# Products in 64-row tiles beside a windowed attention, sums of v in 64x32 tiles, and queues listed by hand

## The chip, the cores and the metric

One core of a Trainium2 chip runs the whole kernel as one program. The metric is the device time in microseconds, the median of three runs. All tensors are float32. The wide products use the fp32r form, in which a float32 operand is split beforehand into a high part (hi) and a rest (lo) and a product is the sum of three (hi*hi, hi*lo, lo*hi); the program lists them as TERMS.

## The reference

```python
x = A_x                                            # 2048 rows of 512
g = sigmoid((x * gate_w).sum(-1, keepdims=True))
a_ = x @ dft_hid_re.T ; b_ = x @ dft_hid_im.T      # 512 x 512 each
a = dft_seq_re @ a_ - dft_seq_im @ b_              # 2048 x 2048 each
qkv = x @ wqkv                                     # 32 heads of 16 columns
scores = q @ k.T * 0.25                            # query i sees keys i-255 .. i
b = softmax(scores) @ v @ wo
out = g * a + (1 - g) * b
```

## The kernel before

**Wide products.** Every product that is not attention has 128 contracted rows, 128 columns of weights and 512 streamed columns. Projections of q, k and v (`qk_proj`, `v_proj`) and the hidden transform (`ab_proj`) take 12 such products for one result of 128x512 in PSUM; the sequence transform (`c_block`, `c_half`, line 534) takes 48 for each of 16 row blocks, first with the real matrix, then with the imaginary one. The matrices come in 64 pieces of 128x1024, loaded by SP's queue into `raw` and split into `hi` (a cast) and `lo` (a subtraction) in halves of 512 columns by "jobs" that are dealt out one by one between the products. Results of the first half of the transform go to DRAM (`r_scr`) and are loaded again to be added to the second (`add`, `add_r`). In all these are 2490 products of 512 columns.

**Attention.** Heads go in 4 groups of 8; queries and keys in 32 blocks of 64 a group, so 128 blocks n. In each, 4 pairs of heads p. `s_pair` (line 372) takes the 64 queries of two heads as 128 weight columns: `make_pad` (lines 353, 355) copies them with zeros into `pad`, so that the heads stay apart in the contraction; 320 keys stream by. VectorE adds the mask and takes the row's extreme (line 374), ScalarE takes the exponential and its row sum (line 377). Maxima go through a transpose (`ml_split`, `ml_turn`, `ml_rows`) and DRAM into extra rows of `ring`, so that `t_pair` (line 454), 19 blocks later (LAG), makes the same scores transposed, key rows by query columns, with the maximum already taken off; ScalarE takes the exponential into `pt` (line 455) and GpSimd clears what lies outside the window (lines 459, 463). Every 4 to 6 blocks `pv` (line 480) sums v over the keys in 128x32 tiles, four column tiles beside one another, in plain float32, for which the profile has two records an instruction; v is spread with zeros into `vpad` by GpSimd (line 437). The sums are divided by the row sums when they leave PSUM (line 501).

**End.** `wo_begin` and `wo_end` multiply the attention's output with wo by a scheme with seven products of 128x256 columns for each pair of row blocks (line 929, 336 instructions), between the last blocks of the transform.

**What sets the order.** TensorE's order is the program's own: the loop over n puts S, T and two rations of `fill` (steps of the generator `dense`, one wide product each) behind one another. The other engines' instructions are ordered by the tile scheduler's timeline model, held in places by `behind`. PSUM has 8 banks: four for `s` and `t` (pool `ps_a`, one bank each), two for `o`, two for the wide products.

```python
ps = ps_a.tile([P, 512], F32, name="s", tag="st")                                          # 371
nc.tensor.matmul(ps[:, :w], PAD[0, n][:, p], ring[1][:, p, k0:k0 + w], start=True, stop=True)   # 372
```

Of the kernel before, what the change touches and what calls it, by code (L numbers as in the profile page):

```python
# [19 lines left out]
NP = 4  # L20
BQ = 64
NB = S // BQ
WIN = 320
BIG = 1e30
SCALE = 0.25
LAG = 19
WARM = 10
SWITCH = 6
FILL_FIRST, FILL_PAIR, FILL_T = 3.0, 4.0, 3.0
# [3 lines left out]
def fnet_window_mix(ctx: ExitStack, tc: tile.TileContext, xT, x, wqk, wv, wr, wi, cr, ci, wo, gw, out):  # L33
# [4 lines left out]
    st = ctx.enter_context(tc.tile_pool(name="st", bufs=3))  # L38
    ev = ctx.enter_context(tc.tile_pool(name="ev", bufs=5))
# [6 lines left out]
    qk_scr = [[[dram.tile([2, P, 512], F32, name=f"qk_scr{i}_{g}_{c}") for c in range(4)]  # L46
               for g in range(NG)] for i in range(2)]
    v_scr = [dram.tile([2, P, 2, NG, 64], F32, name=f"v_scr{i}") for i in range(8)]
    ab_scr = [[dram.tile([P, 2, D], F32, name=f"ab_scr{i}_{c}") for c in range(n)] for i, n in enumerate((4, 16))]
    m_scr = [dram.tile([4, NP, 512], F32, name=f"m_scr{i}") for i in range(16)]  # L50
    l_scr = [dram.tile([NP, 2, 512], F32, name=f"l_scr{i}") for i in range(16)]
    o_scr = [dram.tile([NG, P, 512], F32, name=f"o_scr{i}") for i in range(4)]
    r_scr = [[dram.tile([P, D], F32, name=f"r_scr{i}_{c}") for c in range(16)] for i in range(3)]

    def ld(dst, src):
        mark("sp", nc.sync.dma_start(dst, src))

# [4 lines left out]
    last = {}  # L62

# [3 lines left out]
    @contextmanager  # L67
    def behind(*engines):
        with ExitStack() as es:
            for e in engines:  # L70
                if e in last:
                    es.enter_context(tc.issue_after(last[e]))
            yield
# [13 lines left out]
    def split_psum(hi, lo, ps, scale=1.0):  # L87
        mark("act", nc.scalar.activation(hi, ps, AF.Copy, scale=scale))
        if scale == 1.0:
            mark("dve", nc.vector.tensor_sub(lo, ps, f(hi)))  # L90
        else:
            mark("dve", nc.vector.scalar_tensor_tensor(lo, ps, scale, f(hi), op0=OP.mult, op1=OP.subtract))
# [3 lines left out]
    def load_raw(src):  # L96
        raw = st.tile([P, 1024], F32, name="raw", bufs=2)
        ld(raw, src)
        return raw
# [9 lines left out]
    ended = []  # L109
# [1010 lines left out]
```

## Time and profile before

| | |
|---|---|
| runs (us) | 844.39, 843.87, 844.32; median 844.32 |
| profiled execution | span 841.8 us from its first to its last instruction, 2.5 us under the median of the runs (no time of its own is listed beside the span) |
| TensorE (PE) | 837.9 us busy, granted clock full throughout |
| VectorE (DVE), ScalarE (ACT), GpSimd (POOL) | 643.1, 610.1, 294.9 us busy |
| transfers | 161.03 MB, SP's queue 58.9% of the 16 engines' span |

A product's duration in the profile (393 ns for 512 columns) overlaps the next product's; what counts on the path is the distance from start to start. The chain of waits follows the last instruction back, and its shares add up to the span.

### The profile page before, as it was taken

The page shows a single profiled execution, that of the slowest core. Times are in us where ns is not written, and L with a number is a line of the kernel's source. Part 1 is how long each engine was busy: PE and PEld are TensorE (multiplying, and loading weights), DVE is VectorE, ACT ScalarE, POOL GpSimd, SP SyncE. Part 2 cuts the span into 40 slices and gives each one's busy share as a digit, 9 for nine tenths or more (in the row PEclk, how much of TensorE's full clock was granted, in tenths as well). Part 3 has the DMA queues.
Part 4 walks back from the last instruction along what each step waited for, and adds up shares of the span by engine and source line. Part 5 has one row for each costly group of instructions (what it writes and reads, how often), then busy time and mean ns, then how long its engine had stood idle before and what let it go on. Part 6 is the DMA issues. An engine that isn't in the chain of part 4 may idle for free.

```text
span 841.8 us, 17198 instructions
## 1 busy us (share of the span) xinstructions
PE 837.9 (100%) x5322; PEld 698.4 (83%) x5322; DVE 643.1 (76%) x2084; ACT 610.1 (72%) x1832; POOL 294.9 (35%) x604
## 2 busy tenths in 40 slices
PE   9999999999999999999999999999999999999998
PEld 8888888888888888888888887878888878878997
DVE  5588977777879787787877876878987867656974
ACT  6488888878888897787877877867877865553330
POOL 8101333233332233342323243343143357756410
PEclk9999999999999999999999999999999999999999
DMA  8776678485756183533454557969864256456632
GB/s 301 249 225 205 209 237 282 158 273 194 231 206 197 46 235 111 175 116 122 140 163 124 167 160 221 299 217 317 277 200 155 96 175 196 143 195 203 206 133 93
DMA packets 94491, 161.03 MB, mean 191 GB/s; under 512 B 26816, under 2 KB 35520, under 8 KB 94400
## 3 DMA queue, kind: packets, MB, share of 16 engines
q1 hardware_dynamic: 93968, 159.28, 58.9%
q8 instruction: 42, 0.69, 0.3%
q10 hardware_dynamic: 432, 0.66, 0.2%
q14 instruction: 49, 0.40, 0.1%
HBM read 108.27 MB, written 51.64 MB: 190 GB/s over the span
## 4 chain that ended last, share of the span: by engine, by line
PE 100%; DVE 0%; issue 0%
PE dc L534 42%; PE dab L309 11%; PE dqk L286 10%; PE t L454 9%; PE s L372 9%; PE o L480 8%; PE dv L309 5%; PE t L929 5%; PE s L274 1%; PE dv L599 1%; PE s L392 0%; PE t L564 0%; DVE rt L566 0%
## 5 line engine op out<-in xcount | busy, mean ns | idle before, releaser
L534 PE MATMUL dc<-big,hi 128*128 128x512 f32 x1020 | 344.3, 393 | 0.0
L374 DVE CUSTOM_DVE_ANT_0 sm<-s,mask 128x320 f32<-128x320 f32 (+4 forms) x512 | 235.1, 464 | 111.0 <-PE s L372 71.1
L377 ACT ACTIVATE sm<-sm,ml 128x320 f32<-128x320 f32 (+4 forms) x512 | 277.3, 543 | 56.2 <-DVE ml L374 52.4
L455 ACT ACTIVATE pt<-t 128x320 f32<-128x320 f32 (+4 forms) x392 | 159.5, 411 | 83.5 <-PE t L454 78.2
L534 PE MATMUL dc<-big,lo 128*128 128x512 f32 x510 | 200.0, 392 | 0.0
L534 PEld LDWEIGHTS dc<-big,hi 128*128 128x128 f32 x1020 | 179.4, 188 | 21.2
L459 POOL TENSOR_SCALAR_AFFINE_SELECT pt<-pt 128x128 f32<-128x128 f32 x196 | 75.7, 386 | 278.2 <-ACT pt L455 276.1
L454 PE MATMUL t<-ring,pad 128*128 128x320 f32 (+4 forms) x512 | 156.6, 306 | 0.0
L372 PE MATMUL s<-ring,pad 128*128 128x320 f32 (+4 forms) x512 | 155.0, 303 | 0.0
L355 DVE TENSOR_SCALAR pad<-ring,half 96x256 fp32r<-96x256 f32 x384 | 118.7, 356 | 5.2 <-PE t L454 4.9
L454 PEld LDWEIGHTS t<-ring,pad 128*128 128x128 f32 x512 | 96.0, 188 | 30.4 <-issue 8.7
L372 PEld LDWEIGHTS s<-ring,pad 128*128 128x128 f32 x512 | 96.2, 188 | 20.3 <-DVE ml L374 0.7
L534 PEld LDWEIGHTS dc<-big,lo 128*128 128x128 f32 x510 | 95.9, 188 | 11.9
L593 DVE TENSOR_TENSOR lo<-raw,hi 128x512 fp32r<-128x512 f32 x139 | 95.9, 697 | 2.5 <-ACT hi L593 2.4
L377 ACT ACTIVATION_READ_ACCUMULATOR sm<-sm,ml 128x1 f32 x512 | 97.3, 190 | 0.0
L309 PE MATMUL dab<-hi,big 128*128 128x512 f32 x256 | 88.9, 394 | 0.0
L286 PE MATMUL dqk<-big,hi 128*128 128x512 f32 x240 | 85.0, 393 | 0.0
L437 POOL TENSOR_SCALAR vpad<-vr,half 128x256 f32<-128x256 f32 x64 | 62.1, 981 | 60.4 <-PE o L480 29.5
L353 ACT ACTIVATE pad<-ring,half 96x256 fp32r<-96x256 f32 x128 | 66.8, 522 | 0.0
L459 POOL TENSOR_SCALAR_AFFINE_SELECT home<-home 128x128 f32<-128x128 f32 x60 | 33.9, 565 | 89.8 <-ACT home L455 85.3
L463 POOL TENSOR_SCALAR_AFFINE_SELECT pt<-pt 128x128 f32<-128x128 f32 x172 | 63.0, 366 | 0.0
L593 DVE CAST hi<-raw 128x512 fp32r<-128x512 f32 x126 | 53.9, 435 | 11.9 <-PE dc L534 10.6
(121 smaller groups left out, 1034.0 us busy)
## 6 DMA issues: line engine op xcount, KB each, us to landing
qk_scr<-home SPq DMA_DIRECT2D x32, 512.0 KB
ring<-qk_scr SPq DMA_DIRECT2D x32, 512.0 KB
raw<-cr SPq DMA_DIRECT2D x32, 512.0 KB
raw<-ci SPq DMA_DIRECT2D x32, 512.0 KB
r_scr<-ev SPq DMA_DIRECT2D x42, 256.0 KB
ab_scr<-home SPq DMA_DIRECT2D x20, 512.0 KB
big<-ab_scr SPq DMA_DIRECT2D x20, 512.0 KB
ring<-qk_scr SPq DMA_DIRECT2D x32, 256.0 KB
```

The lines of the kernel that those rows point to most:

```text
L286: nc.tensor.matmul(ps, w[a][:, c:c + 128], XT[dk, ss][:, b], start=n == 0, stop=n == 11)
L309: nc.tensor.matmul(ps, XT[dk, ss][:, a, c * 128:(c + 1) * 128], wh[b], start=n == 0, stop=n == 11)
L355: mark(f"pad{i}", nc.vector.tensor_scalar(dst, src, half[:96, h:h + 1], None, op0=OP.mult))
L372: nc.tensor.matmul(ps[:, :w], PAD[0, n][:, p], ring[1][:, p, k0:k0 + w], start=True, stop=True)
L374: mark("dve", nc.vector.tensor_tensor_reduce(out=sm[:, :w], in0=ps[:, :w], in1=mask[:, WIN - w:], scale=1.0, scalar=3e38, op0=OP.add, op1= ...
L377: mark("act", nc.scalar.activation(sm[:, :w], sm[:, :w], AF.Exp, bias=nm[:, c], scale=-1.0, accum_out=l[:, c]))
L454: nc.tensor.matmul(ps[:, :w], PAD[1, n][:, p], ring[0][:, p, q0:q0 + w], start=True, stop=True)
L455: nc.scalar.activation(pt[:, p, :w], ps[:, :w], AF.Exp, scale=-1.0)
L459: nc.gpsimd.affine_select(a, a, pattern=[[0, 2], [2, 64]], compare_op=OP.is_ge, fill=0.0, base=1, channel_multiplier=-1)
L480: nc.tensor.matmul(OT[g, sb][32 * p:32 * p + 32, q - sb * 512:e - sb * 512], v2[:, p], pt[:, p, q - q0:e - q0], start=first, stop=kb == 8 ...
L534: nc.tensor.matmul(ps, w[a][:, i % 8 * 128:i % 8 * 128 + 128], ab[SC[i]][:, b], start=i == ends[0] and a + b == 0, stop=i == ends[1] and a ...
L593: return fn(*args)
```

## The change

**Tiles of the wide products.** From the q and k projections of rows 1024 on to the seventh block of the second transform, `product` issues each wide product as two of 64 contracted rows, `lhs[r]` and `rhs[r]` with r the rows 0-63 or 64-127. `halves64` pairs them: at step t the upper half of one result, and beside it the lower half of another result, in another bank, from an order that is rotated and 6 steps late (DELAY). A result is ready when both halves are through. Between the halves a `tick`, a ScalarE copy of one column of the bank, orders them. 24 products at the start, 96 behind them and 426 at the end (LATE: the last nine blocks, `c_block`) keep 128 rows; 1944 are halved.

**Attention.** Blocks are of 128 queries or keys, 8 groups of 4 heads, LAG 9 blocks. Each head has 48 rows of `ring` at partition 0 or 64 (its 16 columns three times, as hi or lo), with the maxima behind them in two more; the scores of two heads are two products of 64 rows (384 columns, two banks of one PSUM tile), with no `pad`. S keeps only the extreme (VectorE writes the scores to `junk`); its exponential and row sum are gone. T takes one exponential of 128x768 for two heads. `pv` sums v in 64x32 tiles (64 keys, 16 columns of v and 16 ones, which give the row sums); two halves of keys go to two banks, ScalarE copies both out (`o_evict`), VectorE adds them, and the inverse row sums travel through DRAM (`l_move` to `l_back`) before GpSimd multiplies (`o_mul`).

**Queues.** All five engines' orders are now the program's: `agenda` lists by quarter block when each step is issued, `due` by product steps. Of the transforms' inputs 50 pieces, x, weights and the copies of the hidden transform are loaded by GpSimd's queue; 21 of the first transform's partial results are added in DRAM by accumulating transfers, in place of a load and an add. The hidden transform's results are stored once as float32 and split again after loading (`load_ab`). `hi` casts of pieces go to ScalarE, `lo` to VectorE, after attention to GpSimd. PSUM: two tiles of two banks (`ps_a`) for S, T, `o` and the transposes, four banks for wide products. SWITCH goes from 6 to 7. The first pair's copy of a wo product is VectorE's instead of ScalarE's.

```diff
-LAG = 19
+LAG = 9
+VISIT = 4
+DELAY = 6
+LATE = 9
-    ps_a = ctx.enter_context(tc.tile_pool(name="ps_a", bufs=4, space=PSUM))
-    ps_o = ctx.enter_context(tc.tile_pool(name="ps_o", bufs=2, space=PSUM))
-    ps_d = ctx.enter_context(tc.tile_pool(name="ps_d", bufs=2, space=PSUM))
+    ps_a = ctx.enter_context(tc.tile_pool(name="ps_a", bufs=2, space=PSUM))
+    ps_d = ctx.enter_context(tc.tile_pool(name="ps_d", bufs=4, space=PSUM))
...
     def s_pair(n, p):
...
-        ps = ps_a.tile([P, 512], F32, name="s", tag="st")
-        nc.tensor.matmul(ps[:, :w], PAD[0, n][:, p], ring[1][:, p, k0:k0 + w], start=True, stop=True)
-        sm = at.tile([P, WIN], F32, name="sm", bufs=3)
-        mark("dve", nc.vector.tensor_tensor_reduce(out=sm[:, :w], in0=ps[:, :w], in1=mask[:, WIN - w:],
...
-        mark("act", nc.scalar.activation(sm[:, :w], sm[:, :w], AF.Exp, bias=nm[:, c], scale=-1.0,
-                                         accum_out=l[:, c]))
+        ps = ps_a.tile([P, 2, 512], F32, name="s", tag="st")
+        for h in range(2):
+            r = slice(64 * h, 64 * h + 48)
+            nc.tensor.matmul(ps[:, h, :w], ring[0][r, p, j * P:j * P + P], ring[1][r, p, k0:k0 + w],
+                             start=True, stop=True)
+        for h in range(2):
+            c = p * 8 + h * 4 + jj
+            mark("dve", nc.vector.tensor_tensor_reduce(out=junk[:, :w], in0=ps[:, h, :w], in1=mask[:, WIN - w:],
...
     def t_pair(n, p):
...
-        nc.tensor.matmul(ps[:, :w], PAD[1, n][:, p], ring[0][:, p, q0:q0 + w], start=True, stop=True)
-        nc.scalar.activation(pt[:, p, :w], ps[:, :w], AF.Exp, scale=-1.0)
+        ps = ps_a.tile([P, 2, 512], F32, name="t", tag="st")
+        for h in range(2):
+            r = slice(64 * h, 64 * h + 50)
+            nc.tensor.matmul(ps[:, h, :w], ring[1][r, p, q0:q0 + P], ring[0][r, p, q0:q0 + w],
+                             start=True, stop=True)
+        ph = slice(2 * p, 2 * p + 2)
+        nc.scalar.activation(pt[:, ph, :w], ps[:, :, :w], AF.Exp, scale=-1.0)
...
-            for p in range(NP):
-                nc.tensor.matmul(OT[g, sb][32 * p:32 * p + 32, q - sb * 512:e - sb * 512], v2[:, p],
-                                 pt[:, p, q - q0:e - q0], start=first, stop=kb == 8 * sb + 7,
-                                 skip_group_check=True)
+        for n, pair in enumerate(pairs):
+            for h, (kb, _) in enumerate(pair):
+                a, e = spans[kb, h]
+                r = slice(64 * h, 64 * h + 64)
+                v = vt[(4 * G + kb // 4) % 3]
+                for j in range(HG):
+                    nc.tensor.matmul(o[32 * j:32 * j + 32, h, a - q0:e - q0], v[r, kb % 4, 32 * j:32 * j + 32],
+                                     PT[G * NB + kb][r, j, a - kb * P:e - kb * P],
+                                     start=n == 0, stop=n == len(pairs) - 1, skip_group_check=True)
...
+    def product(part, half, i):
...
+        r = slice(64 * half, 64 * half + 64)
+        nc.tensor.matmul(o.ps, lhs[r], rhs[r], start=start, stop=end and o.left == 0, skip_group_check=True)
+        if end:
+            if o.left:
+                nc.scalar.copy(tick, o.ps[:, 0:1])
+            else:
+                o.end(o)
+    def halves64(groups):
+        first = [(p, i) for g in groups for p in g for i in range(p.n)]
+        second = [(p, i) for g in groups for p in [g[-1], *g[:-1]] for i in range(p.n)]
...
+        for t in range(len(first) + DELAY):
...
+                product(part, 0, i)
+            if t >= DELAY:
+                part_b, i_b = second[t - DELAY]
+                product(part_b, 1, i_b)
+            if t < len(first):
+                job(i + 1)
+            beat()
+            yield
...
+            after(STORE, add_pool if tb in sent else ld, r_scr[0][tb], t)
...
-        nc.scalar.copy(u, p1)
+            after(1, nc.scalar.copy if i else nc.vector.tensor_copy, u, p1)
```

TensorE in the middle of the run, before: S and T (lines 372, 454) alternate behind two transform products each.

```order
L372 MATMUL s_6956<-ring1_265,pad0_1_261 128x320
L534 MATMUL dc_6901<-big_3725,hi_6804 128x512
L534 MATMUL dc_6901<-big_3725,lo_6805 128x512
L454 MATMUL t_6964<-ring0_264,pad1_0_262 128x320
L534 MATMUL dc_6901<-big_3791,hi_6804 128x512 x2
L372 MATMUL s_6969<-ring1_265,pad0_1_261 128x320
```

The same stage in the changed kernel; d_5604 and d_4964 are two results whose upper and lower halves go side by side (line 553), and the two heads of S or T are the row with x2 (lines 373, 432).

```order
L373 MATMUL s_5611<-ring1_270,ring0_269 128x384 x2
L553 MATMUL d_5604<-big_4211,lo_5339 128x512
L553 MATMUL d_4964<-big_5151,lo_5228 128x512
L553 MATMUL d_5604<-big_4275,hi_5338 128x512
L553 MATMUL d_4964<-big_5185,hi_5227 128x512
```

One more pair with the names of the last two rows follows, and then T: where two whole products stood between S and T, three pairs of half products or four stand now.

TensorE at a visit of `pv`, before (two results o, since 64-key blocks cross the border of 512 queries):

```order
L480 MATMUL o_4438<-pt_4538,vpad0_299 32x320 x4
L480 MATMUL o_4438<-pt_4598,vpad1_300 32x256 x4
L480 MATMUL o_4894<-pt_4598,vpad1_300 32x64 x4
L480 MATMUL o_4438<-home_304,vpad1_300 32x192 x4
L480 MATMUL o_4894<-home_304,vpad1_300 32x128 x4
```

and now, one result a visit, with equal widths for the two halves of rows:

```order
L467 MATMUL o_4126<-pt_3877,vt0_286 32x320 x8
L467 MATMUL o_4126<-pt_3942,vt0_286 32x256 x4
L467 MATMUL o_4126<-pt_3700,vt2_288 32x256 x4
L467 MATMUL o_4126<-pt_3700,vt2_288 32x192 x4
L467 MATMUL o_4126<-pt_3942,vt0_286 32x192 x4
L467 MATMUL o_4126<-pt_3999,vt0_286 32x128 x4
L467 MATMUL o_4126<-pt_3636,vt2_288 32x128 x4
```

The number of such instructions in the whole program is twice what it was (1408 against 704), each with half the rows; visits go from 25 to 32.

VectorE before, between two S reductions (line 374; 355 is a pad):

```order
L593 CAST hi_5593<-raw_5501 128x512
L374 ISA sm_5659,ml_5233<-s_5657,mask_266 128x320
L374 ISA ml_5233 128x1
L593 TENSOR_TENSOR lo_5594<-raw_5501,hi_5593 128x512
L355 TENSOR_SCALAR pad0_1_261<-ring0_264,half_283 96x4x64 x2
L355 TENSOR_SCALAR pad1_0_262<-ring1_265,half_283 96x256
L374 ISA sm_5674,ml_5233<-s_5672,mask_266 128x320
```

and now, at a place where three subtractions of 512 columns (line 111 for a result of the hidden transform, 161 for a piece) stand between the last reduction of one S and the first of the next:

```order
L377 ISA ml_4632 128x1
L111 TENSOR_TENSOR big_4628<-d_4448,big_4628 128x512
L161 TENSOR_TENSOR lo_4578<-raw_4306,hi_4577 128x512
L111 TENSOR_TENSOR big_4659<-d_4520,big_4659 128x512
L377 ISA junk_283,ml_4632<-s_4672,mask_271 128x384
```

The pads and casts have left VectorE's list, and the order of what is left is fixed.

More of the change, by code (lines that the diff above doesn't have):

```diff
@@ new lines, in v_evict, with store, load_ab, cast @@
+    def v_evict(sb, ps):
+        t = ev.tile([P, 512], F32, name="ev")
+        nc.scalar.copy(t, ps)
+        def store():
+            ld(v_scr[sb // 4][sb % 4], t)
+            have.add(("v", sb))
+        after(STORE, store)
+    STAGE = []
+    def load_ab(i, sc, into):
+        if not STAGE:
+            t = const.tile([P, 6, 512], F32, name="stage", tag="home")
+            STAGE.extend(t[:, k] for k in range(6))
+        STAGE.append(STAGE.pop(0))
+        raw = STAGE[-1]
+        ld_pool(raw, ab_scr[i][sc])
+        def cast():
+            t = into[sc] = big.tile([P, 2, 512], F32R, name="big")
+            nc.scalar.copy(t[:, 0], raw)
+            after(3, nc.vector.tensor_sub, t[:, 1], raw, f(t[:, 0]))
+        after(SPLIT_AB, cast)
@@ new lines, in v_whole @@
+        def v_whole(sb):
+            ps = ps_d.tile([P, 512], F32, name="d", tag="d")
+            yield from whole(row_ops(sb, wvs), ps)
+            v_evict(sb, ps)
+            yield
+        x_soon(1)
+        for sb in range(4):
+            yield from v_whole(sb)
+        x_soon(2)
+        for i in range(2):
+            ps = ps_d.tile([P, 512], F32, name="d", tag="d")
+            yield from whole(qk_ops(1, i, wq0), ps)
+            qk_evict(0, 1, i, ps)
+            yield
+        for sb in (4, 5):
+            yield from v_whole(sb)
@@ L755, in dense @@
[L755 to L765 removed]
+            load_ab(1, sc, nxt)
@@ new lines, in dense, with to_c, load_r, add_r @@
+        c_groups = [[c_get(k) for k in g] for g in keys]
+        def to_c():
+            for sc in range(4):
+                after(8 * sc, load_ab, 0, sc, ab)
+        c_groups[0][0].mid[12] = to_c
+        yield from halves64(groups + c_groups)
+        have.add("halves")
+        def load_r(tb):
+            return mixed.pop(tb, None) if tb > 13 else fetch(r_scr[0][tb])()
+        def add_r(tb, ps, r):
+            nc.vector.scalar_tensor_tensor(r, ps, g1[:, tb:tb + 1], r, op0=OP.mult, op1=OP.add)
+            after(STORE, ld, out[tb] if tb > 13 else r_scr[1][tb], r)
@@ L767, in fnet_window_mix @@
+        for tb in range(16 - LATE, 16):
+            yield from c_block(pieces, tb, nxt, load_r, add_r) if tb < 15 else c_final(pieces, nxt)
+    steps = []
+    taken = [0]
     FIN = []
[L768 to L769 removed]
     mixed = {}
[L771 to L785 removed]
@@ L972, in need @@
             next(stream)
[L974 to L988 removed]
+    EACH = [(h, i) for h in range(2) for i in range(2)]
```

1187 lines of the change are left out of this document (577 added, 610 removed).

## The prediction

> **What bounds the kernel now.** I read the page's first two parts, then the chain of waits, then the order of time on TensorE.
>
> ```profile
> span 841.8 us, 17198 instructions
> PE 837.9 (100%) x5322; PEld 698.4 (83%) x5322; DVE 643.1 (76%) x2084; ACT 610.1 (72%) x1832; POOL 294.9 (35%) x604
> PEclk9999999999999999999999999999999999999999
> ```
>
> The chain of waits, by line:
>
> ```profile
> by line: PE dc L534 41.8%; PE dab L309 10.5%; PE dqk L286 9.8%; PE t L454 9.0%; PE s L372 8.6%; PE o L480 8.1%; PE dv L309 5.3%; PE t L929 4.8%; PE s L274 0.7%; PE dv L599 0.5%; PE s L392 0.2%; PE t L564 0.2%; DVE rt L566 0.1%; issue 0.0%
> ```
>
> TensorE works without a gap at full clock, and the path is TensorE's from end to end. So the time moves with the sum of TensorE's work and with any wait that it gets; what other engines save is worth nothing by itself. Busy time hides how long one product holds the path, so I take distances between starts. Middle of the run, then the end, TensorE's products:
>
> ```profile
> 400.15 0.31 PE L372 MATMUL s<-ring,pad 128*128 128x320 f32 x1
> 400.29 0.39 PE L534 MATMUL dc<-big,hi 128*128 128x512 f32 x1
> 400.52 0.39 PE L534 MATMUL dc<-big,lo 128*128 128x512 f32 x1
> 400.75 0.31 PE L454 MATMUL t<-ring,pad 128*128 128x320 f32 x1
> ```
> ```profile
> 827.97 3.04 PE L929 MATMUL t<-ring 128*128 128x256 f32 x24
> 830.85 0.63 PE L534 MATMUL dc<-big,hi 128*128 128x512 f32 x2
> ...
> 833.59 0.64 PE L929 MATMUL t<-ring 128*128 128x256 f32 x4
> ```
>
> 24 products of 256 columns take 830.85 - 827.97 = 2.88 us, 0.120 each; the 12 of 512 columns behind them take 2.74 us, 0.228 each. So 256 columns cost 0.108, and some 0.012 us of each product doesn't depend on its width. 320 columns take 0.14 (400.15 to 400.29).
>
> **The change, part by part.**
>
> *Scores S and T.* The chain gives S 8.6% and T 9.0% of 841.8: 148.2 us for 1024 products of up to 320 columns. Now there are 256 units each of S and T, a unit being two products of 64 rows that should run beside one another: 224 of 384 columns, 16 of 256, 16 of 128. On the line through 0.120 and 0.228, 384 columns cost 0.174 and 128 cost 0.066: 2 x (224 x 0.174 + 16 x 0.120 + 16 x 0.066) = 83.9 us. This saves 64.3, because blocks of 128 queries waste fewer columns of the window (384 for 128, not 320 for 64) and no pad rows fill the array. If the two products of a unit did not overlap at all, the units would cost 167.8.
>
> *Wide products.* Lines 534, 309, 286 and 274 hold 68.1% of the chain, 573 us for 2490 products, 0.230 each. 1944 become pairs of halves with the same columns. No row shows two row tiles side by side; the nearest are the sums of v, four column tiles side by side:
>
> ```profile
> L480 PE MATMUL o<-pt,vpad 128*32 128x320 f32 x400 | 31.4, 436 | 0.0
> L480 PE MATMUL o<-pt,vpad 128*32 128x64 f32 x168 | 6.2, 219 | 0.0
> 0.00:842.00 842.00, 70.06 (x1408) 38.55 (x1408) 1.00 0.60 191
> ```
>
> The third row is line 480 alone over the whole span: TensorE busy, its loads busy, clock, share of the DMA engines, GB/s. In the first, 400 x 0.436 = 174 us of products fit in 31.4: tiles do overlap, here across columns. I take a pair at the price of the whole product, so 0. Lower end: the pair hides the fixed 0.012, 1944 x -0.012 = -23 us. Upper end: no overlap, 1944 x 0.228 = +443 us. The value lies near the lower end, as the rows above do.
>
> *Weight loads.* A pair needs two loads where a product needed one:
>
> ```profile
> 400.15 0.19 PEld L534 LDWEIGHTS dc<-big,hi 128*128 128x128 f32 x1
> 400.30 0.19 PEld L534 LDWEIGHTS dc<-big,lo 128*128 128x128 f32 x1
> 400.52 0.19 PEld L454 LDWEIGHTS t<-ring,pad 128*128 128x128 f32 x1
> ```
>
> The second load begins 0.01 us after the product at 400.29 on the same rows, and the next product starts at 400.52: a load runs under the product before it. Line 480 has 1408 loads in 38.55 us, 0.027 each, where the loads of one whole tile here are 0.15 apart at the closest: loads of different tiles run together too. So I add nothing. The Trainium skill, in "TensorE: Matmul & The Clock Gate" (Part 3, what overlaps and what doesn't), says that a load overlaps products in flight only where its row group differs. By that rule a tile's own load would stand in the open; the trace disagrees with the 0.01 us above, and what the rule would give is among the rivals.
>
> *Sums of v.* The work is the same 176 steps, of eight tiles instead of four: 68.2 us stay (8.1%). Lower end 0. Upper end: the narrowest group takes 6.2 / 168 = 0.037 us a record; if records set the pace, 2816 records take 104, +36. I take +1, since the wide group shows the tiles, not the records, to set it.
>
> *Changes of tile shape.* A visit to the sums of v costs an entry and an exit:
>
> ```profile
> 248.00 0.39 PE L309 MATMUL dab<-hi,big 128*128 128x512 f32 x1
> 248.31 2.36 PE L480 MATMUL o<-pt,vpad 128*32 128x320 f32 x32
> 250.60 0.38 PE L454 MATMUL t<-ring,pad 128*128 128x256 f32 x1
> L454 PE MATMUL t<-ring,pad 128*128 128x256 f32 x16 | 4.7, 294 | 0.0
> ```
>
> Entry: 0.31 instead of 0.23; exit: that T is 0.38 long where its form has 0.294. Some 0.17 a visit, 7 more visits: +1. Wide products and scores share one shape now, so the 1944 pairs bring no changes of their own. The transposes (line 392, 0.2%) keep 32 short steps: 0.
>
> *VectorE and the new wait.* Its rows and those of the engines that take over work:
>
> ```profile
> L374 DVE CUSTOM_DVE_ANT_0 sm<-s,mask 128x320 f32<-128x320 f32 x448 | 215.0, 485 | 91.4 <-PE s L372 55.6 <-ACT sm L377 26.9 <-ACT home L88 1.9
> L374 DVE CUSTOM_DVE_ANT_0 sm<-s,mask 128x256 f32<-128x256 f32 x16 | 6.6, 419 | 2.8 <-PE s L372 1.8 <-ACT sm L377 0.9
> L355 DVE TENSOR_SCALAR pad<-ring,half 96x256 fp32r<-96x256 f32 x384 | 118.7, 356 | 5.2 <-PE t L454 4.9
> L593 DVE TENSOR_TENSOR lo<-raw,hi 128x512 fp32r<-128x512 f32 x139 | 95.9, 697 | 2.5 <-ACT hi L593 2.4
> L593 DVE CAST hi<-raw 128x512 fp32r<-128x512 f32 x126 | 53.9, 435 | 11.9 <-PE dc L534 10.6 <-DMA raw<-ci 1.3
> L455 ACT ACTIVATE pt<-t 128x320 f32<-128x320 f32 x344 | 145.4, 427 | 68.3 <-PE t L454 63.4 <-PE s L372 3.9
> L455 ACT ACTIVATE pt<-t 128x256 f32<-128x256 f32 x12 | 4.6, 382 | 5.9 <-PE t L454 5.6
> L377 ACT ACTIVATE sm<-sm,ml 128x320 f32<-128x320 f32 (+4 forms) x512 | 277.3, 543 | 56.2 <-DVE ml L374 52.4
> L459 POOL TENSOR_SCALAR_AFFINE_SELECT pt<-pt 128x128 f32<-128x128 f32 x196 | 75.7, 386 | 278.2 <-ACT pt L455 276.1 <-PE s L372 1.0 <-DMA ring<-qk_scr 0.7
> L593 POOL TENSOR_TENSOR lo<-raw,hi 128x512 fp32r<-128x512 f32 x3 | 3.9, 1297 | 0.0
> ```
>
> Pads (118.7) and casts (53.9) leave VectorE; 448 reductions grow by 64 columns, 0.066 each (0.485 - 0.419), +30. So VectorE drops to some 520 us, 32 additions for the sums of v counted in, and ScalarE, which loses 277 and takes on some 142 casts, to less than its 610. Neither is the bound. But scores had four banks and now have two tiles, used in turn: the next S unit needs the tile of this one. In between TensorE has some six pairs and two units, 6 x 0.23 + 2 x 0.174 = 1.73 us. A unit's products need some 0.33 to end, VectorE's two reductions 2 x 0.551 = 1.10: 0.30 are left, and VectorE is free for 0.63 of the 1.73, about one subtraction of 0.697. Of the 255 gaps between S units in VectorE's order, 29 without a visit hold two operations of 512 columns and 7 hold three: late by 0.76 and 1.46, less 0.30: 29 x 0.46 + 7 x 1.16 = 21 us at most, 0 at least (the neighbours, often empty, and a visit's two us of other work catch it up). I take 4. What queues behind a late S on TensorE is everything: its order is fixed.
>
> T's tile: 0.33 and one exponential of 768 columns, 0.427 + 448 x 0.0007 = 0.74; 0.66 are left. The tick copies stand behind at most one of these, and have six steps, about 1.4 us. 0.
>
> *GpSimd and transfers.* Two more rows, the last transfer that SP issues and the page's count of transfers:
>
> ```profile
> 838.70 0.33 SPq L567 DMA_DIRECT2D out<-rt  x1
> DMA packets 94491, 161.03 MB, mean 191 GB/s; under 512 B 26816, under 2 KB 35520, under 8 KB 94400
> ```
>
> 480 selections over twice the elements (0.386 to 0.772 each, 185 to 371 us), 57 operations of 1.3 us and 114 transfers to issue, whose price on this engine no row shows (SP's last issue took 0.33; up to 1.3, its longest operation here, makes 38 to 148). Even the upper ends add up to under 600 of 785 us. The last selection before a visit has four quarter blocks, over 3 us, and TensorE would wait if a transfer's issue stood before it: 0 to 32 visits x 1 us; I take 1.
>
> 161 MB stay about 161: a third copy of the keys' and queries' columns and doubled sums of v come, the halved copies of the hidden transform and 21 loads go. Loads of partial results start 42 steps ahead, over 10 us of products; if that cover were short, ps_d's banks would wait, 256 KB at 191 GB/s being 1.4 us. 0 taken, 0 to +10. The end keeps its 128-row products, and the first copy's engine is worth nothing there: TensorE doesn't wait for it in the chain.
>
> Sum on the span: 841.8 - 64.3 + 0 + 1 + 1 + 4 + 1 = 784.5. The runs' median is 2.5 above the span: 787.
>
> **Rivals.**
>
> - *Loads queue* (slower). If the two tiles' loads went one after the other, a pair would take 2 x 0.15 = 0.30, +0.07 x 1944 = +136, and the 512 units 0.30 for 0.174, +64: 987. For it: PEld is busy 83% with one load a product. Against: 0.027 a load at line 480. It decides from +0.029 a pair on (57 / 1944). Chance 0.07.
> - *A tile's load isn't hidden under its own product*: 0.15 more for each pair and unit, 2456 x 0.15 = +368: 1155. For it only the half-height tiles, which no row shows. Chance 0.02. This is the rule of the Trainium skill named above.
> - *Row tiles don't overlap* (the change doesn't do what it says): +443 and +84: 1314. Chance 0.02.
> - *Waits for the two tiles of scores* eat the gain: with 0.1 to 0.2 us a unit of S, 813 to 838; at 0.22 nothing is left. For it the 0.30 us of room and the fixed order, against it VectorE's falling load. Chance 0.15 (806 to 842), and 0.02 that it ends within 0.2% of before, which is about what a measurement can tell from no change.
> - *Pairs shed the fixed part*: 764. Chance 0.10.
>
> The forecast (770 to 806) has 0.62. Faster 0.62 + 0.15 + 0.10 = 0.87, same 0.02, slower 0.11. The range 766 to 828 holds the forecast, the upper part of the pairs that shed (0.06) and most of the waits (0.12): 0.80.
>
> **What would show it.** Right: half products (line 553) start in twos, pairs 0.23 apart; S and T (lines 373, 432) about 0.17 on the path, some 10% of the chain together; line 467 near 70 us; VectorE's and ScalarE's busy time lower. Wrong: pairs over 0.26 apart (loads), TensorE's weight loads waiting for VectorE's line 377 (tiles of scores) or for GpSimd before line 467, or a chain that leaves TensorE.

## The result, and the profile after

The changed kernel takes 837.48 us (median of four runs, 836.13 to 838.83) against 844.1 us: ratio 0.9922, 95% interval 0.9908 to 0.9936. It is faster, by 6.6 us or 0.8%, where 57 were forecast; its profiled execution has a span of 836.0 us where the sum came to 784.5. The first parts of its page:

```profile
span 836.0 us, 22632 instructions
PE 812.6 (97%) x8706; PEld 663.9 (79%) x8706; DVE 536.3 (64%) x1523; ACT 442.2 (53%) x834; POOL 383.5 (46%) x697
PE 16%; DMA 5%; DVE 2%; issue 1%; SPq 1%; ACT 1%; POOL 0%; DVEq 0%; ACTq 0%; POOLq 0%
```

TensorE, 837.9 of 841.8 us busy before, now stands still for 23 us, and the third row, the chain by engine, leaves TensorE: that was the last of the signs named for a wrong forecast. (Its shares add up to 26% here: in this profile the chain is followed back only through the last 220 us, so the stages before are read from waits and distances.) Who is late stands in the list of waits (engine, line and what it waits for; us in all, times, longest):

```profile
PEld s L373 <- DVE ml L377: 18.1, 42, 1.4
PEld o L467 <- issue: 10.5, 26, 1.4
PEld s L393 <- DVE ml L377: 8.2, 18, 1.1
PEld t L1023 <- DVE rt L1028: 7.8, 16, 1.0
PE t L1023 <- DVE ex L145: 3.0, 1, 3.0
```

S and the transposes (lines 373, 393) wait for VectorE's reductions (line 377), the wo products (line 1023) for VectorE's additions; the second row, for the sums of v, names nobody. What the parts became is read from distances between TensorE's starts, less the prices of the prediction (0.228 for 512 columns, 0.120 for 256, and the line through them). I summed this over both traces ("dense" is a wide product, or a pair of halves that stands for one):

| us | before | after | more |
|---|---|---|---|
| gaps ahead of S, T, transposes and sums of v | 2.3 | 22.2 | 19.9 |
| products that start late behind such a unit | 2.6 | 9.2 | 6.6 |
| dense product behind dense product | 7.2 | 17.9 | 10.7 |
| products of wo and those ahead of them | 0 | 9.4 | 9.4 |
| the sums of v themselves, exits included | 68.4 | 71.9 | 3.5 |
| the start | 2.9 | 3.9 | 1.0 |

That is 51.1 us, of which the forecast held 7. The other part of the miss is that S and T fell by 58.4 at these prices and not by 64.3. Of the 1.5 us that are left of the 51.5 between sum and span, 1.4 are six steps more: the halves' list ends DELAY steps late, 6 x 0.228. One of the longest gaps, on TensorE and then on VectorE (start, duration, line, tiles, count; in brackets the idle time before):

```profile
210.15 0.62 PE L553 MATMUL d<-big,hi 64*128 64x512 f32 x4
210.61 0.39 PE L553 MATMUL d<-big,lo 64*128 64x512 f32 x2
211.93 0.44 PE L373 MATMUL s<-ring,ring 48*128 48x384 f32 x2 [0.93 <-DVE ml L377]
212.21 0.63 PE L553 MATMUL d<-big,hi 64*128 64x512 f32 x4
212.67 0.39 PE L553 MATMUL d<-big,lo 64*128 64x512 f32 x2
```
```profile
208.92 0.69 DVE L111 TENSOR_TENSOR home<-d,home 128x512 fp32r<-128x512 f32 x1
209.52 0.68 DVE L161 TENSOR_TENSOR lo<-raw,hi 128x512 fp32r<-128x512 f32 x1
210.12 0.68 DVE L113 SCALAR_TENSOR_TENSOR home<-d,home 128x512 fp32r<-128x512 f32 x1
210.72 0.55 DVE L377 CUSTOM_DVE_ANT_0 junk<-s,mask 128x384 f32<-128x384 f32 x1
211.31 0.56 DVE L377 CUSTOM_DVE_ANT_0 junk<-s,mask 128x384 f32<-128x384 f32 x1
```

The S at 209.06 is reduced at 210.72 to 211.9, since three operations of 512 columns stand ahead of it; the next S needs its tile and starts at 211.93 instead of 210.84. Its successor starts 0.28 behind it, not 0.174, because its load could not run ahead: it starts 0.11 us behind S (212.04), where behind a T that doesn't wait, at 196.53, both start together. At 212.21 four half products start in 0.46 us: pairs do overlap, 0.23 each, as forecast.

### The profile page after: what moved, and what is told of

It is laid out like the page before. It is cut to its first block, busy times and chain, and to the rows that moved or that the text cites. A ratio compares the mean times of both kernels' runs of the same rounds, so it can differ in the third digit from the quotient of the medians.

```text
span 836.0 us, 22632 instructions
## 1 busy us (share of the span) xinstructions
PE 812.6 (97%) x8706; PEld 663.9 (79%) x8706; DVE 536.3 (64%) x1523; ACT 442.2 (53%) x834; POOL 383.5 (46%) x697
## 5 line engine op out<-in xcount | busy, mean ns | idle before, releaser
L377 DVE CUSTOM_DVE_ANT_0 junk<-s,mask 128x384 f32<-128x384 f32 (+2 forms) x512 | 271.8, 531 | 165.3 <-PE s L373 154.0
L553 PE MATMUL d<-big,hi 64*128 64x512 f32 x1920 | 347.6, 396 | 1.3 <-ACT tick L556 1.3
L437 POOL TENSOR_SCALAR_AFFINE_SELECT pt<-pt 128x256 f32<-128x256 f32 x256 | 124.2, 485 | 323.4 <-ACT pt L435 262.9
L435 ACT ACTIVATE pt<-t 128x768 f32<-128x768 f32 (+2 forms) x256 | 197.7, 772 | 105.4 <-PE t L432 103.5
L553 PEld LDWEIGHTS d<-big,hi 64*128 64x128 f32 x1920 | 194.5, 186 | 25.5 <-ACT tick L556 1.7
L553 PE MATMUL d<-big,lo 64*128 64x512 f32 x960 | 206.7, 395 | 0.0
L553 PE MATMUL d<-hi,big 64*128 64x512 f32 x672 | 135.8, 396 | 0.0
L553 PEld LDWEIGHTS d<-big,lo 64*128 64x128 f32 x960 | 100.2, 186 | 12.5 <-issue 0.5
L441 POOL TENSOR_SCALAR_AFFINE_SELECT pt<-pt 128x256 f32<-128x256 f32 x224 | 96.1, 429 | 0.0
L606 PE MATMUL dc<-big,hi 128*128 128x512 f32 x284 | 92.1, 393 | 0.0
L467 PE MATMUL o<-pt,vt 64*32 64x320 f32 (+4 forms) x2816 | 74.2, 348 | 3.1 <-DVE ml L377 2.9
L606 PEld LDWEIGHTS dc<-big,hi 128*128 128x128 f32 x284 | 52.7, 189 | 9.0 <-issue 0.4
```

The costliest lines, as they stand in the source:

```text
L377: mark("dve", nc.vector.tensor_tensor_reduce(out=junk[:, :w], in0=ps[:, h, :w], in1=mask[:, WIN - w:], scale=1.0, scalar=3e38, op0=OP.add, ...
L435: nc.scalar.activation(pt[:, ph, :w], ps[:, :, :w], AF.Exp, scale=-1.0)
L437: nc.gpsimd.affine_select(a, a, pattern=[[0, 2], [1, P]], compare_op=OP.is_ge, fill=0.0, base=0, channel_multiplier=-1)
L441: nc.gpsimd.affine_select(a, a, pattern=[[0, 2], [-1, P]], compare_op=OP.is_gt, fill=0.0, base=0, channel_multiplier=1)
L467: nc.tensor.matmul(o[32 * j:32 * j + 32, h, a - q0:e - q0], v[r, kb % 4, 32 * j:32 * j + 32], PT[G * NB + kb][r, j, a - kb * P:e - kb * P] ...
L553: nc.tensor.matmul(o.ps, lhs[r], rhs[r], start=start, stop=end and o.left == 0, skip_group_check=True)
```

## Experiments

Times are medians, ratios those to the kernel before; the changed kernel stands at 837.5 and 0.9922.

**Short reductions.** The softmax is the same for whatever value is subtracted, so a maximum over fewer keys leaves nothing out of the result; only its guard against overflow is weaker.

```diff
-            mark("dve", nc.vector.tensor_tensor_reduce(out=junk[:, :w], in0=ps[:, h, :w], in1=mask[:, WIN - w:],
+            k = slice(128, 192) if w == WIN else slice(0, w)
+            mark("dve", nc.vector.tensor_tensor_reduce(out=junk[:, k], in0=ps[:, h, k], in1=mask[:, WIN - w:][:, k],
```

> S's two reductions read 64 of the 384 columns (the extreme is taken over those alone, the rest is left out), so that VectorE gives each tile of scores back sooner; TensorE's list is the same. Theory 1 (TensorE waits for the two shared PSUM tiles because VectorE's reductions come late): the gaps ahead of line 373, most of those ahead of line 393 and some ahead of 467, together about 20 us of the changed kernel, go, and with them some 5 us of products that start late behind such a wait: 837.5 falls to 810 to 820. Theory 2 (the 50 us are the price of the pairs and of the tile shapes, and the gaps are only where it shows): 834 to 838.

824.5 us, ratio 0.9768 (0.9741 to 0.9795): 13 us less than the changed kernel, and faster than both, though above theory 1's 810 to 820. The group of the reductions, and then the longest waits of TensorE (line numbers are one or two higher here):

```profile
L378 DVE CUSTOM_DVE_ANT_0 junk<-s,mask 128x64 f32<-128x64 f32 (+2 forms) x512 | 123.2, 241 | 262.2 <-PE s L373 245.0 <-PE d L555 7.5
```
```profile
PEld o L469 <- issue: 13.4, 32, 1.9
PEld t L1025 <- DVE rt L1030: 6.6, 15, 1.1
PEld t L434 <- ACT pt L437: 6.0, 4, 4.1
```

No S waits for VectorE any more: the gaps between a pair and S fell from 9.3 to 1.7 us, those ahead of transposes to nothing. Theory 1 holds. By the same sum over the trace (of the longest of the four runs, 828.4 us) the gaps ahead of S, transposes and sums of v and the late starts behind them are some 19 us less; the gaps ahead of T are 4 more and the sums of v themselves 4.5. One wait holds most of what was taken back: T waited once for ScalarE, which stood at an eviction:

```profile
218.67 0.60 ACT L107 ACTIVATE home<-d 128x512 fp32r<-128x512 f32 x1 [4.67 <-DMA qk_scr<-home]
220.53 0.69 PE L434 MATMUL t<-ring,ring 50*128 50x384 f32 x2 [3.70 <-ACT pt L437]
221.02 0.63 PE L555 MATMUL d<-big,lo 64*128 64x512 f32 x2
```

Behind this gap a pair takes 0.42 us (221.02 to 221.44), nearly twice its time: the granted clock is 0.50 from 220.5 to 226.5 us, and the visit to the sums of v that falls into it takes 4.2 us where 2.4 is the median.

**Clusters, or the reductions' length.** A cluster is two or more operations of 512 columns in VectorE's list between the reductions of one S and those of the next. Three runs took such work out of the way. First, holding it back on VectorE (`vec` puts a closure into a queue that is emptied behind S's reductions, 12 steps later at the latest; stores of q and k 18 instead of 11 steps behind):

```diff
-        after(4, low)
+        after(4, vec, low)
...
+        vec_gap()
```

> Nothing is left out: VectorE's subtractions and additions of 512 columns (lines 111, 113, 145, 161, 265, 478) are held back so that mostly one, seldom two, stand between the reductions of one S and the next (gaps with two or more of them: 19 for 50). Theory 1a (the reductions are late because of clusters of such work, three of 0.69 us being more than the 1.7 us between two S): 817 to 828. Theory 1b (they are late because two reductions of 0.53 us and TensorE's own 0.33 are too long for the two tiles): 834 to 838. If subtractions that come later hold up products, 838 to 845.

852.3 us, ratio 1.0096. Held operations may read buffers that have been given on, so the values are others; and products waited for results that came later (line 578 there, the half products, waits 5.8 and 3.8 us for VectorE's lines 111 and 113, which it hardly does in the changed kernel). That is the third outcome, beyond its 838 to 845, and tells nothing of clusters. Second, handing 52 operations to GpSimd:

```diff
-            after(3, nc.vector.tensor_sub, t[:, 1], raw, f(t[:, 0]))
+            after(3, nc.gpsimd.tensor_sub, t[:, 1], raw, f(t[:, 0]))
-        nc.vector.tensor_add(OT[i], OT[i], ots[:, 2])
+        nc.gpsimd.tensor_add(OT[i], OT[i], ots[:, 2])
```

> Nothing is left out: 32 additions for the sums of v (line 478) and 20 subtractions of reloaded hidden-transform results (line 145) go from VectorE to GpSimd, so that of the gaps between two S on VectorE 29 instead of 50 hold two or more operations of 512 columns. Theory 1a (such clusters make S wait): 21 of 50 clusters go, and some 6 to 8 us of the 17 us that shorter reductions took from the rows ahead of TensorE's products: 829 to 832. Rival (GpSimd's additions of 1.3 us slow VectorE's while both run, 1.4 against 0.69 us in the trace, and stand in front of the selections that the sums of v wait for): 836 to 842.

845.7 us, ratio 1.0016 (0.9998 to 1.0035): 8 us slower than the changed kernel, and above the rival's range. Its waits, then the group of VectorE's subtractions (busy us, mean ns) in it and in the changed kernel, and one such subtraction with what GpSimd does at that time, from the changed kernel's timeline:

```profile
PEld s L373 <- DVE ml L377: 16.3, 35, 1.3
PEld s L393 <- DVE ml L377: 12.5, 19, 2.1
```
```profile
L161 DVE TENSOR_TENSOR lo<-raw,hi 128x512 fp32r<-128x512 f32 x117 | 100.1, 856 | 44.9 <-ACT hi L160 39.8 <-PE t L432 5.0
```
```profile
L161 DVE TENSOR_TENSOR lo<-raw,hi 128x512 fp32r<-128x512 f32 x117 | 90.7, 776 | 34.5 <-ACT hi L160 31.9 <-PE t L432 2.4
```
```profile
320.19 1.48 DVE L161 TENSOR_TENSOR lo<-raw,hi 128x512 fp32r<-128x512 f32 x1
319.82 1.29 POOL L499 TENSOR_TENSOR ev<-ots,ev 128x512 f32<-128x512 f32 x1
```

The rival's mechanism shows. Of the 117 subtractions 39 run with GpSimd idle, at 0.68 us each, and 22 beside a GpSimd operation on two tensors, at 1.36; in the changed kernel it is 46 and 11 (the last two rows show one). T waits more too: by the same sum the gaps ahead of it are 8.3 us, for 3.2. The Trainium skill, "SBUF — State Buffer" (Who interferes with whom), says that a VectorE instruction with two SBUF inputs and a GpSimd instruction that reads SBUF exclude one another; these numbers agree for operations on two tensors. Beside GpSimd's selections the subtractions take 0.74 to 0.78 in the mean. Third, the same 52 operations without GpSimd: the additions for the sums of v are left out (half of the keys is missing), the subtractions become ScalarE copies.

```diff
-            after(3, nc.vector.tensor_sub, t[:, 1], raw, f(t[:, 0]))
+            after(3, nc.scalar.copy, t[:, 1], raw)
-        nc.vector.tensor_add(OT[i], OT[i], ots[:, 2])
+        pass
```

> The same 52 operations leave VectorE's list as when GpSimd took them, but GpSimd gets nothing: the 32 additions for the sums of v are left out (so one half of the keys is missing from the sums), the 20 subtractions become ScalarE copies of the unsplit values. Theory 1a (clusters on VectorE make S wait; GpSimd's operations beside VectorE's ate the gain before): 829 to 833. Theory 1b (the reductions' own length in the two tiles' cycle): 835 to 838.

833.1 us, ratio 0.9873 (0.9857 to 0.9890).

```profile
PEld s L373 <- DVE ml L377: 9.9, 27, 1.1
PEld s L393 <- DVE ml L377: 7.3, 17, 1.1
```

With 29 for 50 clusters the waits of S fell from 42 to 27 and the gaps between a pair and S from 9.3 to 5.7 us. Clusters are a part of it (theory 1a, just above its 829 to 833): 4.4 us for these 52 operations, where short reductions gave 13.

**Whole products in place of pairs.** The upper half's instruction takes all 128 rows, the lower half's is gone.

```diff
-        nc.tensor.matmul(o.ps, lhs[r], rhs[r], start=start, stop=end and o.left == 0, skip_group_check=True)
+        if half == 0:
+            nc.tensor.matmul(o.ps, lhs, rhs, start=start, stop=end, skip_group_check=True)
```

> The 1944 pairs of halves become 1944 whole products of 128 rows, in the place of the upper half; S and T stay in 64-row tiles. If half-height pairs cost more than whole products (0.233 against 0.228, some at 0.33) and a change of the array's shape costs nothing, 10 to 20 us are gained: 818 to 828. If each change between 128-row and 64-row tiles costs what a visit to line 467 shows (0.09 in, 0.10 out), 512 units of S and T add 512 x 0.19 = 97 us: 915 to 930. My theory is the second, with half the price at units whose neighbours overlap: 880 to 930.

1015.3 us, ratio 1.2017 (1.1996 to 1.2038), far above even my own range. One S among whole products:

```profile
400.50 0.39 PE L551 MATMUL d<-big,hi 128*128 128x512 f32 x1
400.82 0.44 PE L373 MATMUL s<-ring,ring 48*128 48x384 f32 x2
401.19 0.50 PE L551 MATMUL d<-big,hi 128*128 128x512 f32 x1
401.52 0.39 PE L551 MATMUL d<-big,lo 128*128 128x512 f32 x1
401.75 0.62 PE L551 MATMUL d<-big,hi 128*128 128x512 f32 x2
```

The distances are 0.32, 0.37, 0.33 where the prices are 0.228, 0.174, 0.228: 0.09 ahead of S, 0.20 behind it, 0.10 behind the next product, 0.39 in all; times 512 units, 200 us. The Trainium skill, "TensorEngine Tiling (Array Packing)" (Key Properties), says that changing the tiling mode drains TensorE; it gives no time, and this is one. Next, S and T as 128-row products too (each sums both heads' scores, so the values are others):

```diff
-            r = slice(64 * h, 64 * h + 48)
+            r = slice(0, 128)
-            r = slice(64 * h, 64 * h + 50)
+            r = slice(0, 128)
```

> As the run with whole products, but S and T are issued as 128-row products too (each sums the scores of both heads, so the values are others), so nothing but the sums of v and the transposes changes the array's shape. A unit of S or T then costs two products, 2 x 0.174: 83.9 us more for 512 units. Theory 6 (a pair costs 0.006 more than a whole product, 12 us for 1944, and the longer cycle takes most of S's waits, some 15): 837.5 + 84 - 12 - 15 = 894, 888 to 900, and 115 to 125 us less than the whole products beside 64-row S and T. Rival (pairs cost what whole products cost, and the waits stay): 907 to 921.

909.0 us, ratio 1.0769 (1.0750 to 1.0787). One T there:

```profile
399.94 0.39 PE L552 MATMUL d<-big,lo 128*128 128x512 f32 x1
400.17 0.51 PE L433 MATMUL t<-ring,ring 128*128 128x384 f32 x2
400.51 0.63 PE L552 MATMUL d<-big,hi 128*128 128x512 f32 x2
400.98 0.40 PE L552 MATMUL d<-big,lo 128*128 128x512 f32 x1
```

My theory 6 falls. A whole product behind a whole product takes 0.238 us here in the mean (1368 distances, median 0.233), a pair behind a pair 0.238 in the changed kernel (1240, median 0.233): a pair costs what a whole product costs at the same place. In the kernel before it was 0.233 in the mean (1468, median 0.228). So products became 0.005 dearer in the new program, halved or not, but only while attention runs: behind the last sums of v the median is 0.227 in both of the new traces, and so it is among the whole products ahead of the first S. The cause is open. 909 is 84 for the doubled units, less some 12 where shorter waits are the likely reason: the gaps ahead of attention's products are 13 us here, against 22.

**The end.** Two runs moved the first wo pair or its loads:

```diff
-FIRST_OUT, PAIR = 104, 38
+FIRST_OUT, PAIR = 116, 38
```

> The first pair of the wo products starts 12 steps later (FIRST_OUT 116 for 104), some 2.7 us, all other pairs too. Theory 3 (the end's gaps ahead of line 1023, 7 us in all, come from the attention's last output, which travels through DRAM and GpSimd's sums and is late for the first pair alone): the gap of 3.4 us at 708 us goes, and the products at half clock behind it: 832 to 835. Rival (every pair's VectorE additions or loads are late by themselves): the later gaps stay or grow, 836 to 839.

842.2 us, ratio 0.9974 (0.9964 to 0.9984): slower than the changed kernel and above both ranges; the first gap grew from 3.4 to 5.5 us and a second of 3.8 followed.

```diff
-            ld(t.rearrange("p (g t) -> p g t", g=NG),
+            (nc.scalar.dma_start if i == 0 else ld)(t.rearrange("p (g t) -> p g t", g=NG),
```

> The loads of the first wo pair (tw from o_scr) are issued by ScalarE's queue instead of SP's, where they stand behind transfers of the attention's last outputs that wait for VectorE and GpSimd. Theory 3a (the 3.4 us gap at 708 us is this queue's order: these loads are issued too late): the gap shrinks by 2 to 3 us and with it the products at half clock behind it: 832 to 835. Rival 3b (the loads wait for their buffer or for the attention's own data, whatever the queue): 836 to 840.

838.2 us, ratio 0.9935: the gap shrank to 2.1 us and another of 2.5 came 6 us later. With the partial results early as well and on ScalarE's queue:

```diff
-            for n, fn in ((-54, wo_load), (-36, wo_sums), (-16 if i == 7 else -30, r_load)):
+            for n, fn in ((-54, wo_load), (-36, wo_sums), (-16 if i == 7 else -50 if i == 0 else -30, r_load)):
...
-                ld(t, r_scr[int(i != R15 and tb >= 16 - LATE)][tb])
+                (nc.scalar.dma_start if i == 0 else ld)(t, r_scr[int(i != R15 and tb >= 16 - LATE)][tb])
```

> As the run with the first pair's loads on ScalarE's queue, and the first pair's partial results (rt from r_scr) too, issued 20 steps earlier. Theory 3c (the end's 7 us ahead of line 1023 are two late loads one behind the other: without the first the second, rt, is what VectorE waits for, 3.5 us in that run): both gone, 832 to 835. Rival 3b' (the end is held by ScalarE's casts and GpSimd's sums, which stand in list order behind loads of ci and of the attention's last output): 836 to 839.

835.6 us, ratio 0.9895 (0.9881 to 0.9910; the changed kernel's interval begins at 0.9908), between the two ranges. From the first to the last product of the nine last blocks it takes 147.9 us in this trace, 147.4 in the changed kernel's: nothing was gained there, and theory 3 is borne out in none of its forms. Then VectorE's additions at the end were cut to 32 columns, the rest left out:

```diff
+            r, t = r[:, :32], t[:, :32]
             nc.vector.scalar_tensor_tensor(r, t, g, r, op0=OP.mult, op1=OP.add)
-            after(3, into, r2.rearrange("p (n e) -> p n e", n=2), u2.unsqueeze(1).to_broadcast([P, 2, 256]), gb)
+            after(3, into, r2, u2, gb)
```

> At the end VectorE's additions of the wo products to the results (line 1028) take 32 columns of 256 or 512, the rest is left out; TensorE's and all other lists are the same. From the first to the last product of the last nine blocks the changed kernel takes 147.4 us where its products alone would take 426 x 0.228 + 336 x 0.120 = 137.4, and loads issued early moved its waits without shortening it (147.9, 147.1). Theory 7 (the 10 us are VectorE's: products wait for these additions, 16 times in the list of waits): 139 to 142 us for the stretch, 830 to 833 in all. Rival (loads, casts and GpSimd's sums hold it): 146 to 148 and 836 to 839.

832.2 us, ratio 0.9856 (0.9839 to 0.9874), and the stretch takes 142.0 us. Of the 16 waits for these additions one is left (line 1029 is 1028):

```profile
PEld t L1023 <- DVE rt L1029: 1.8, 1, 1.8
```

So 4 to 5 of the end's 10 us are VectorE's additions: of the 5.4 us less, up to 1.7 may be the clock, which fell to half for 3.4 us in the changed kernel's end and didn't here. What is left stands mostly at the first pair: its second group of products waits 2.8 us here. That this pair's inputs come late is argued from the lists; no run removed it.

**The smaller edits.** The last line of the diff undone, so that ScalarE makes the first copy of the first wo pair:

```diff
-            after(1, nc.scalar.copy if i else nc.vector.tensor_copy, u, p1)
+            after(1, nc.scalar.copy, u, p1)
```

> The last edit of the change alone is undone: the first copy of the first pair of wo products goes back from VectorE to ScalarE. Mine: it moves nothing by itself, 836 to 839, because the first pair waits 3 us for its operands before there is anything to copy. Rival (VectorE's list is what makes the end late): 834 or less; or (ScalarE's list holds a cast that waits for a load in front of the copy, which was the reason to move it): 840 to 844.

840.6 us, ratio 0.9964 (0.9951 to 0.9977): 3 us slower, by the second rival. ScalarE's list at that place, and TensorE's wait:

```profile
714.51 0.62 ACT L160 CAST hi<-raw 128x512 fp32r<-128x512 f32 x1 [4.83 <-DMA raw<-ci]
715.04 0.36 ACT L145 COPY ex<-t 128x256 f32<-128x256 f32 x1
715.46 1.65 PE L1023 MATMUL t<-fin,ring 128*128 128x256 f32 x6 [7.43 <-ACT ex L145]
```

The copy stands behind a cast that waits 4.8 us for its load. The smallest of all edits holds 3 of the 6.6 us that the change gained. Loads of pieces and weights on SP's queue:

```diff
-        (ld if on_sp else ld_pool)(raw, src)
+        ld(raw, src)
```

> All loads of matrices and weights that GpSimd issues (pieces, wqk, wi, wr; 0.55 to 0.65 us of GpSimd each) go to SP's queue, as in the kernel before. Mine: the queue moved nothing for TensorE, 835 to 840. Rival 4a (the issues delay GpSimd's selections and so the sums of v): 830 to 834. Rival 4b (SP's queue holds them behind stores that wait): 845 or more.

842.9 us, ratio 0.9984 (0.9957 to 1.0010), runs from 836.5 to 848.5: unclear in size, between my expectation and rival 4b. The profiled execution has one gap of 5.2 us at 568 us ahead of T, behind a ScalarE cast that waits for a load from GpSimd's queue.

**Together.** All with short reductions. Stores of q and k earlier, then the multiplication of line 499 on VectorE, then sums of the edits:

```diff
-STORE, STORE_HL = 10, 11
+STORE, STORE_HL = 10, 6
```
```diff
-        nc.gpsimd.tensor_mul(rl, ot, rl)
+        nc.vector.tensor_mul(rl, ot, rl)
```

> Shortened reductions as before (the extreme of 64 of 384 columns), and the results of the q and k projections are stored to DRAM 6 steps behind their last product instead of 11. Theory 5 (the one long gap of the run with short reductions, 3.9 us ahead of T at 216 us, and the half clock behind it, come from ScalarE standing at an eviction, line 107, whose buffer's store was issued late, with T's exponential behind it in ScalarE's list): 4 to 6 us less, 818 to 821. Rival (the store waits for VectorE's rest anyway, or another wait follows): 823 to 827.

826.7 us, ratio 0.9799 (0.9779 to 0.9820): the gap at 216 us went, one of 3.5 came at 226, where T waits for the maxima's load. The rival.

> Shortened reductions, and the 32 multiplications of the attention's output by the inverse row sums (line 499, 1.29 us each on GpSimd) on VectorE. If VectorE's subtractions that take 1.38 us beside a GpSimd operation on two tensors, for 0.68 alone, hold TensorE (about 8 of them stand beside line 499 in the run with short reductions), 2 to 5 us less than 824.5: 819 to 822. Rival (off the path once the reductions are short; or VectorE now stands in front of the reductions waiting for l_scr's load, up to 13 us in GpSimd's list): 824, or 830 and more if these waits reach S.

842.0 us, ratio 0.9951. VectorE's own wait, and TensorE's behind it:

```profile
DVE ev L501 <- DMA ev<-l_scr: 35.7, 11, 8.7
PE s L373 <- DVE ml L378: 15.3, 3, 6.4
```

VectorE stood 35.7 us at this multiplication waiting for the sums' way through DRAM, and the reductions stood behind it: the rival again.

> Short reductions, stores of q and k 6 steps behind, line 499 on VectorE and the end's two loads early, all together. If the causes named are separate, the gains add up: 824.5 less 4 (T), 3 (subtractions), 4 (end): 812 to 816. If one wait takes the other's place: 819 to 825. Whatever comes, the pairs' 0.233 us, the changes of shape at the sums of v and the refilling behind them stay, so it doesn't reach the forecast 787.

842.7 us, ratio 0.9963, above both ranges: VectorE stands 27.9 us at the multiplication of line 499, and S waits 11.2 us for reductions, which the run with short reductions alone doesn't show. Short reductions with the early loads at the end:

> Two edits that gained, together: short reductions (824.5 alone) and the end's first two loads early (2 us less than the changed kernel alone). If they are separate, 821 to 824; if the end then waits for something else, 824 to 828.

824.5 us, ratio 0.9772 (0.9754 to 0.9791): no gain over short reductions. And with two of VectorE's block additions (line 859) moved behind the wo pair's, where `t` would fall among its products:

```diff
-        after(2, done, tb, ps, r)
+        t = beats[0] + 2
+        for i in range(8):
+            b = base[0] + FIRST_OUT + PAIR * i
+            if tb < 12 and b - 2 <= t <= b + 20:
+                t = b + 21
+        after(t - beats[0], done, tb, ps, r)
```

> Short reductions, and at the end two of VectorE's additions for whole blocks (line 859) moved behind the wo products' additions (line 1028) with which they collide. Each takes 0.66 us out of a chain of four VectorE operations that TensorE waits for: 822 to 824, against 824.5 with short reductions alone. Rival (the additions that stay are enough to hold the products): 824 to 826.

824.2 us, ratio 0.9766 (0.9752 to 0.9780), in the rival's range. That is short reductions again: 20 us under the kernel before, 13 under the changed one, and the best that the experiments led to.

## Why the prediction was wrong, step by step

- *What bounds the kernel.* Right for the kernel before. But the sum assumed that TensorE stays without a gap, and it was TensorE's 841.8 us without one that hid how late other engines may be.
- *S and T, -64.3.* The mechanism was right: units of two products run side by side, 0.17 to 0.18 apart from the next product where nothing waits. By the distances between starts they fell by 58.4. The chain's shares for these lines (148.2) held more than the products.
- *Wide pairs, 0.* Right: 0.238 a pair, 0.238 a whole product at the same place, and the rivals of queueing loads, unhidden loads and no overlap are out. But products became 0.005 longer than before while attention runs, some 10 us, which no term had; the cause is open.
- *Weight loads, 0.* Right while nothing waits. A unit that waits also loses its successor's early load, 0.09 to 0.10 each time: part of the 6.6 us of late starts.
- *Sums of v, +1, and changes of shape, +1.* Measured: 3.5 for both, line 467 at 74.2 us. That pairs and S share one shape, as the prediction had it, proved decisive: with whole products beside 64-row S each unit would have cost 0.39 more.
- *VectorE and the new wait, +4.* **This is the step that failed.** It named the place, the tiles and the clusters, and gave 0 to 21. The gaps ahead of the users of these two tiles grew by 19.9 us and the starts behind them by 6.6, and short reductions alone gave 13 back. I took 4 because neighbours would catch up. The bound left out the subtractions at twice their time beside GpSimd, the gaps with a visit, where the additions for the sums of v stand, and that transposes and sums of v use the same two tiles and wait too. How the rest divides among these, no run separates beyond the 4.4 us of the clusters.
- *T's tile, 0.* Its gaps grew by 3 to 4 us, the longest behind ScalarE operations; without VectorE's lateness they grew further.
- *GpSimd, +1.* Its selections were cheaper than feared (0.43 to 0.49 us for 0.77), so visits hardly depended on it (3.9 us of waits in the list). What it did to VectorE was not in the term.
- *Transfers, 0.* 163.5 MB came, and pieces on SP's queue gained nothing.
- *The end, 0.* Wrong, by 9.4 us. I argued from the chain of before, where these products lie among others. Here VectorE's additions are 4 to 5 of it, and the copy whose engine I called worth nothing would cost 3 more on ScalarE.
- *The rival "waits for the two tiles of scores eat the gain"* had the right mechanism and a chance of 0.15, with 806 to 842. It needs 0.1 to 0.2 us for each unit of S; the 26.5 us are 0.10 for each of 256, though only some 9 of them stand ahead of S itself. The rest of the way to 836 came from the end and the longer products.

## What to carry to other kernels

When TensorE is the path and its work shrinks, redo the sum for whoever hands buffers back: add up, for each turn of a shared PSUM tile, everything that stands in its releaser's list, by the durations with the neighbours running, and use the upper end of that bound where the order is fixed and there are only two tiles. A shorter operation in the releaser (here a maximum over fewer keys) can be worth more than moving other work away, since work that is moved is late or in the way elsewhere. Price a change of array shape before mixing tile heights in one stream.

## What the runs showed of the hardware that I had not expected

- Two 64-row products between 128-row products cost 0.39 us more than their columns (0.09, 0.20, 0.10), where I had expected 0.19. Over the 512 units it is 0.37 in the mean (1015.3 us against 909.0 less 84).
- A VectorE subtraction of 128x512 takes 0.68 us alone and 1.36 to 1.38 beside a GpSimd operation on two tensors, by the means over the cases above.
- A gap of 2 to 4 us in TensorE's work can cost more than itself. In the changed kernel, ahead of the wo products and behind it:

```profile
707.05 0.88 PE L1023 MATMUL t<-fin,ring 128*128 128x256 f32 x6
711.63 1.34 PE L1023 MATMUL t<-fin,ring 128*128 128x256 f32 x6 [3.00 <-DVE ex L145]
712.76 0.63 PE L606 MATMUL dc<-big,lo 128*128 128x512 f32 x1
713.19 1.05 PE L606 MATMUL dc<-big,hi 128*128 128x512 f32 x2
```

From 712.76 to 713.19 a product of 512 columns takes 0.43 us instead of 0.228, until 715.3; the granted clock is 0.51 from 711.9 to 715.4 us. The length of the gap alone doesn't decide it. The same six products, with the first pair's loads on ScalarE's queue and with the narrow additions:

```profile
708.46 1.49 PE L1023 MATMUL t<-fin,ring 128*128 128x256 f32 x6 [1.73 <-DVE ex L145]
```
```profile
711.90 0.95 PE L1023 MATMUL t<-fin,ring 128*128 128x256 f32 x6 [2.80 <-DVE ex L145]
```

Behind the shorter gap the granted clock is 0.50 from 708.6 to 712.0 us; behind the longer it stays at 1.00. What decides between them, these runs don't show. The Trainium skill, "TensorE: Matmul & The Clock Gate" (Part 1), says that the clock falls to half after an idle window of about 3.4 us; the rows agree in the half, but here it fell behind a gap of 2.1 us from start to start and not behind one of 3.2.
